# Two more chunk pairs of the first FFN in Strassen's form, and half a query chunk ahead of the product with Wo in the second attention

## The chip, the cores and the metric

The kernel runs on one core of a Trainium2 chip. The metric is the time of one execution on the device, in microseconds; before the change the median of three runs is 401.58 us (401.27 to 401.74). Engines are named as in the profile: PE is TensorE's matmuls and PEld its weight loads, DVE is VectorE, ACT is ScalarE, POOL is GpSimd, SP is SyncE, which issues transfers.

## What is computed

The input x has 2048 tokens of 512 numbers. It goes through an attention block A, a feed-forward block B, A again and B again, with the same weights both times:

```python
def A(x):                                  # 32 heads of 16, linear attention
    q, k, v = split(x @ wqkv)              # wqkv 512 x 1536
    phi = lambda t: where(t > 0, t + 1, exp(t)) + 1e-6
    kv  = einsum("bhsd,bhse->bhde", phi(k), v)
    z   = phi(k).sum(tokens)
    num = einsum("bhqd,bhde->bhqe", phi(q), kv)
    den = einsum("bhqd,bhd->bhq", phi(q), z) + 1e-6
    return (num / den) @ wo
def B(x):                                  # 512 -> 1792 -> 512
    return (silu(x @ w_gate) * (x @ w_up)) @ w_down

x = x + A(layernorm(x)); x = x + B(layernorm(x))
x = x + A(layernorm(x)); x = x + B(layernorm(x))
```

## The kernel before

**Tiling.** Everything stays in SBUF. Tokens are 16 tiles of 128, four tiles to a group (0 to 3). The layers are numbered 0 (first attention), 1 (first FFN), 2 (second attention) and 3 (second FFN). Matmuls read bf16 and add up in eight PSUM banks of 512 columns.

**Tokens of the program.** The string PROGRAM, a table written by hand, is the order of TensorE's work, token by token: layer digit, a letter, and indices. Those that matter here:
- `1u212`: chunk 12 (128 of the 1792 hidden features) of group 2 in layer 1, direct: eight matmuls of 512 columns, four with Wg and four with Wu (`gu`). ACT takes silu of the first bank, DVE multiplies by the second. Late chunks, those behind the first key of layer 2, take the silu by way of tanh, with one more DVE instruction.
- `1y251`: product 1 of 7 of Strassen's form for a pair of chunks, here 5 and 12 (j and j + 7), of group 2 (`gs`). A pair is two chunks by two halves of the group (256 tokens each) by two halves of the 512 inputs; seven products of 4 matmuls of 256 columns (two for the gate, two for up) take the place of 16 matmuls of 512. Products 1, 6 and 7 share one growing bank, which ACT copies out after each (`cp`, line 1248), and products 2, 3 and 5 add a bank to such a copy on DVE (`ca`, line 1227); then ACT takes silu of the gate half (`sih`, line 1219) and POOL multiplies (`hp`, line 1242). Product 4 needs a silu on ACT and a product on DVE (`hh`, line 1258).
- `1p16`: a piece of the product with Wd (`down`), in Strassen's form too, for which DVE adds blocks of h (`1h1.sb1`, line 1322, into RT).
- `2k0`: keys of token tile 0 in layer 2 (four matmuls of 512). `2q10`: query chunk 0 of group 1 (four of 512). `2Q30`: half of query chunk 0 of group 3 early (four of 256, `q_first`); the later `2q30` is then the other half. `U` is the same for an FFN chunk.
- After a query chunk, `phi` runs: ACT's exponential into etmp (`exp`, line 700), DVE's min and add on etmp (`ts`, line 705), and the last step into pq on DVE (`phi`, line 709 or 712), for some chunks after a copy with bias on ACT (`id1`, line 703).
- `2v`: sixteen matmuls of 128 columns that give the masked product of keys and values (`kvt`): the block diagonal is cut out by DVE in two instructions (`mask` and `mask1`, line 809), each for a half, into KVT, which lies in the buffer etmp. `2m0` to `2m3`: that times Wo, one matmul each (`m_mm`); `2m0` and `2m1` need the first half, `2m2` and `2m3` the second.
- `2d10`: a piece of the denominators (Zm by pq, 8 columns); after the fourth, ACT takes the logarithm into dsb and then, for group 1 of layer 2, the reciprocals into rtok (`2d1.rxs`, line 878), which DVE transposes into rT (`2d1.dT`, line 886). `2r1`: sixteen small matmuls with esel that spread them over the features (`rep_pe`); DVE multiplies pq by the result (line 933). For other groups ACT spreads them (`rex`, line 896, into rrep or hT), SP transposes by DMA into RT, and DVE or POOL multiply (`pqn`, line 915). `2w4`: the product of pq with the combined matrix for tile 4 (`wo`).

**Weight pieces.** Strassen's form reads sums of blocks of Wg and Wu (`1W2.ws6` and the like, POOL, line 1101), made once for each two chunks, and sums of blocks of the tokens (`1gx3.xs`). The sums lie where Wqkv and Wo lay. When the last product that reads them is through, `reload` has POOL's queue load Wqkv again in four transfers: two for the keys (`R.ldk`, `R.ldk1`, 256 KB each), one for the queries (`R.ldq`, 512 KB), one for the values (`R.ldv`, 512 KB). The keys of layer 2 read the first two, its queries the third.

**Order of the other engines.** ORDER is a dictionary with one string of operation names for each of ACT, DVE, POOL and SP, written by hand: each engine issues in just that order, and waits for semaphores that the kernel derives from what an operation reads and writes. An operation that waits holds up all that stands behind it on its engine. ON_ACT is a set of names that moves operations between engines.

Of the kernel before, what the change touches and what calls it, by code (L numbers as in the profile page):

```python
# [1588 lines left out]
```

## Time and profile before

| | us |
|---|---|
| median of 3 runs | 401.58 (401.27 to 401.74) |
| the profiled execution | 401.14 |
| its span on the core | 399.4 |
| PE busy | 394.3 (99%) |
| DVE busy | 327.5 (82%) |
| ACT busy | 268.8 (67%) |
| POOL busy | 214.5 (54%) |

The granted clock of TensorE is full (1.00) over the whole span. The profile is of one execution; the 1.7 us between its span and its time lie around the program. The chain of work that ended last is 97% matmuls. A PE row's duration has a modelled end; the start of the next row, where nothing is waited for, tells how long the engine was held.

### The profile page before, as it was taken

Reading aid. Unit: us, or ns where it says so; the run is one execution under the profiler, and the core shown is the slowest. Engines: PE = TensorE matmul, PEld = TensorE weight load, DVE = VectorE, ACT = ScalarE, POOL = GpSimd, SP = SyncE. Lnnn points to the kernel's source line nnn. Section 1 sums busy time; section 2 is a strip of 40 time slices with the busy share of each in tenths; the row PEclk is TensorE's granted clock in tenths of the full one; section 3 lists DMA queues with packets and bytes.
Section 4 is the critical chain, followed back from the end, with each engine's and each line's share of the span. In section 5 each row is a group of like instructions: output and inputs, shape, how many; then the busy total and the mean of one; then the engine's idle time right before and its main releaser. Section 6 shows DMA issues by size and latency. Waiting matters only on the chain.

```text
span 399.4 us, 7922 instructions
## 1 busy us (share of the span) xinstructions
PE 394.3 (99%) x2922; PEld 264.5 (66%) x2922; DVE 327.5 (82%) x785; ACT 268.8 (67%) x569; POOL 214.5 (54%) x352
## 2 busy tenths in 40 slices
PE   7999999999999999999999999999999999999997
PEld 6444555445787787565786445454588888888886
DVE  5996599377987779699997666987698889899997
...
DMA packets 53783, 25.43 MB, mean 64 GB/s; under 512 B 46512, under 2 KB 52144, under 8 KB 53744
## 3 DMA queue, kind: packets, MB, share of 16 engines
...
q10 hardware_dynamic: 544, 0.52, 0.4%
q8 instruction: 23, 0.38, 0.4%
...
## 4 chain that ended last, share of the span: by engine, by line
PE 97%; DMA 1%; DVE 1%; ACT 0%; issue 0%; SPq 0%; DVEq 0%
PE pb L492 97%; DMA X<-in_A_x_dram 1%; DVE pq L1442 0%; PE pb L679 0%; ACT xnA L624 0%; ACT xnA L616 0%; DVE stats L609 0%; DVE etmp L809 0%; SPq L535 0%; DVEq L1559 0%; DVE xnA L655 0%; DVE mv L611 0%; DVE vpe L640 0%; DVE xnA L1368 0%
## 5 line engine op out<-in xcount | busy, mean ns | idle before, releaser
L492 PE MATMUL pb<-xnT,Wg 128*128 128x512 bf16 (+1 forms) x332 | 75.3, 334 | 0.0
L492 PE MATMUL pb<-xnT,Wu 128*128 128x512 bf16 (+1 forms) x332 | 75.3, 334 | 0.0
L1242 POOL TENSOR_TENSOR hT<-pq 128x256 bf16<-128x256 f32 x45 | 34.1, 769 | 45.4 <-ACT pq L1219 45.3
L1248 ACT ACTIVATE pq<-pb 128x512 f32<-128x512 f32 x63 | 36.6, 594 | 28.2 <-PE pb L492 24.8
L492 PEld LDWEIGHTS pb<-xnT,Wu 128*128 128x128 bf16 x332 | 32.5, 98 | 24.2
L1227 DVE TENSOR_TENSOR pq<-pb,pq 128x512 f32<-128x512 f32 x63 | 41.9, 682 | 5.7 <-PE pb L492 2.9
L492 PEld LDWEIGHTS pb<-xnT,Wg 128*128 128x128 bf16 x332 | 32.3, 98 | 21.2 <-DMA xnT<-xnB 0.2
L1018 DVE TENSOR_TENSOR hT<-tht,pb 128x512 bf16<-128x512 f32 x46 | 30.8, 681 | 17.2 <-ACT tht L1013 12.2
L644 POOL TENSOR_TENSOR rstd<-vpe,negh 128x1 f32<-128x1 f32 x62 | 36.5, 590 | 9.5 <-DVE vpe L640 7.3
L1013 ACT ACTIVATE tht<-pb 128x512 f32<-128x512 f32 x46 | 26.4, 594 | 22.5 <-PE pb L492 21.5
L492 PE MATMUL pb<-Wd,hT 128*128 128x256 bf16 x336 | 40.3, 273 | 0.0
L700 ACT ACTIVATE etmp<-pb 128x512 bf16<-128x512 f32 x64 | 36.7, 601 | 3.8 <-PE pb L492 2.9
L492 PEld LDWEIGHTS pb<-Wd,hT 128*128 128x128 bf16 x336 | 32.9, 98 | 4.2
L492 PE MATMUL pb<-pk,xnA 128*128 128x512 bf16 (+1 forms) x152 | 34.7, 362 | 0.0
L492 PE MATMUL pb<-xnT,Wqkv 128*128 128x512 bf16 (+1 forms) x132 | 32.8, 376 | 0.0
L705 DVE TENSOR_SCALAR etmp<-etmp 128x512 bf16<-128x512 bf16 x64 | 19.4, 314 | 15.5 <-ACT etmp L700 15.5
L492 PE MATMUL pb<-Wqkv,xnT 128*128 128x512 bf16 x128 | 30.8, 379 | 0.0
L1219 ACT ACTIVATE pq<-pq 128x256 f32<-128x256 f32 x63 | 24.9, 411 | 8.1 <-DVE pq L1227 8.0
L492 PE MATMUL pb<-GT,pq 128*128 128x512 bf16 x128 | 29.9, 379 | 0.0
L624 ACT ACTIVATE etmp<-X,sums 128x512 bf16<-128x512 bf16 x32 | 22.9, 715 | 5.0 <-DVE X L945 3.8
L628 POOL TENSOR_SCALAR mv<-sums 128x1 f32<-128x1 f32 x52 | 14.1, 275 | 21.2 <-DVE X L945 12.5
L945 DVE SCALAR_TENSOR_TENSOR X<-pb,X 128x512 bf16<-128x512 f32 x32 | 21.1, 681 | 3.5 <-PE pb L492 3.4
...
## 6 DMA issues: line engine op xcount, KB each, us to landing
...
Wqkv<-in_A_wqkv_dram SPq DMA_DIRECT2D x2, 512.0 KB, 7.4
Wo<-in_A_wo_dram POOLq DMA_DIRECT2D x2, 512.0 KB, 4.6
Wqkv<-in_A_wqkv_dram POOLq DMA_DIRECT2D x2, 512.0 KB, 5.1
```

The costliest lines, as they stand in the source:

```text
L492: return op("pe", lambda e: e.matmul(o_ap, lhsT=lhsT, rhs=rhs, start=start, stop=stop, skip_group_check=skip), r=r, w=w, n=n)
L624: op("act", lambda a: a.activation(out=sq_ap, in_=X[:, t, :], func=ACT.Square, scale=-float(D), bias=sums[:, t:t + 1], accum_out=mv[:, t, ...
L644: op("pool", lambda p: p.tensor_tensor(out=rstd[:, t:t + 1], in0=vpe[:, t:t + 1], in1=negh[:], op=ALU.pow), r=[f"vp{t}", "negh"], w=[f"rs{ ...
L700: exps.append(op("act", lambda a: a.activation(out=etmp[e][:], in_=PB[pb], func=ACT.Exp), r=[f"pb{pb}"], w=[f"e{e}"], after=silus, kind="e ...
L705: op("dve", lambda v: v.tensor_scalar(out=etmp[e][:], in0=etmp[e][:], scalar1=1.0, scalar2=1e-6, op0=ALU.min, op1=ALU.add), r=[f"e{e}"], w ...
L945: op("dve", lambda v: v.scalar_tensor_tensor(out=X[:, t, :], in0=PB[pb], scalar=1.0, in1=X[:, t, :], op0=ALU.mult, op1=ALU.add, accum_out= ...
L1013: silus.append(op("act", lambda e: e.activation(out=tht[a][:], in_=PB[pg], func=ACT.Silu), r=[f"pb{pg}"], w=[f"th{a}"], after=exps, kind=" ...
L1018: op("dve", lambda v: v.tensor_tensor(out=hT[h][:, j, :], in0=tht[a][:], in1=PB[pu], op=ALU.mult), r=[f"pb{pu}", f"th{a}"], w=hk, kind="h")
L1219: silus.append(op("act", lambda e: e.activation(out=o_ap, in_=i_ap, func=ACT.Silu), r=r, w=w, after=exps, kind="sih" if len(w) == 1 else " ...
L1227: op("dve", lambda v: v.tensor_tensor(out=c, in0=PB[b], in1=c, op=ALU.add), r=[f"pb{b}", k], w=[k], kind="ca")
L1242: lambda e: e.tensor_tensor(out=hT[h][:, jj, o:o + 256], in0=c[:, 0:256], in1=c[:, 256:512], op=ALU.mult),
L1248: op("act", lambda e: e.activation(out=c, in_=PB[pb], func=ACT.Copy), r=pk_, w=[k], kind="cp")
```

## The change

Four things change, all in tables; no function does.

1. PROGRAM loses the chunks 1u212, 1u205 (group 2), 1u304 and 1u311 (group 3), and gains the fourteen products 1y251 to 1y257 and 1y341 to 1y347, that is the pairs (5, 12) of group 2 and (4, 11) of group 3. They stand between 1u303 and 2k0, woven into what was there; the two chunks of group 3 stood behind 2k0 before. The last product that reads the piece sums in Wqkv's place is 1y343 now; it was 1y243.
2. PROGRAM gains 2Q30 between 2v and 2m0; one bank is held from there until 2q30.
3. The four strings of ORDER get the new operations, and many neighbours change places, in layers 0 and 3 too.
4. ON_ACT gains 1c303, which moves nothing here, since the buffer it needs is lent out.

```diff
-1u303 1y243 1u212 1u306 1u205 1u309 1y301 1y311 1u302 1y306 1u310 1y316 1y315 1y307 1y305 1u313 1y317 1y304 1y302
-1y312 1y303 1y313 1y314 2k0 2k1 2q10 2k4 1u304 2k3 2k2 2k6 1p21 2q01 2k5 1u305 1p26 1p22 1p27 1p25 1u311 1p24 1u312
...
+1u303 1y251 1y243 1y252 1y256 1y345 1u306 1y255 1y257 1y341 1u309 1y253 1y301 1y342 1y254 1y346 1y311 1u302 1y306
+1u310 1y347 1y315 1y316 1y344 1y307 1y343 1y305 1u313 1y317 1y304 1y302 1y312 1y303 1y313 1y314 2k0 2k1 2q10 2k4 2k3
...
-2d22 2d23 2g4 2d11 2d12 2g1 2d13 2q33 2v 2m0 2m1 2m3 2m2 2r1 2w3 2w2 2w0 2w1 2q30 2q32 2w4 2d31 2w6 2w8 2w7 2w10 2d33
+2d22 2d23 2g4 2d11 2d12 2g1 2d13 2q33 2v 2Q30 2m0 2m1
+2m3 2m2 2r1 2w3 2w2 2w0 2w1 2q30 2q32 2w4 2d31 2w6 2w8 2w7 2w10 2d33 2w9 2d30 2d32 2w11 2w5 3U008 3u008 3u001 3u004
...
     "dve": """
-0d0.pqn 0q30.ts 0v.mask 0v.mask1 0q30.phi 0q31.ts 0M2.evac 0q31.phi 0d1.pqn1 0q33.ts 0w1.res 0d2.dT 0w2.res 0q33.phi
+0d0.pqn 0v.mask 0q30.ts 0v.mask1 0q30.phi 0q31.ts 0M2.evac 0q31.phi 0d1.pqn1 0q33.ts 0w1.res 0d2.dT 0w2.res 0q33.phi
```

The first place is TensorE at the masked product of the second attention: GT with Wqkv is 2v, Wo with etmp are 2m0 to 2m3, rT with esel is 2r1. Before:

```order
L492 MATMUL pb<-xnT,Wqkv 128x512 x4
L492 MATMUL pb<-GT,Wqkv 128x128 x16
L492 MATMUL pb<-Wo,etmp 128x512 x4
L492 MATMUL pb<-rT,esel 128x128 x16
L492 MATMUL pb<-GT,pq 128x512 x16
L492 MATMUL pb<-xnT,Wqkv 128x512 x8
```

After:

```order
L495 MATMUL pb<-xnT,Wqkv 128x512 x4
L495 MATMUL pb<-GT,Wqkv 128x128 x16
L495 MATMUL pb<-xnT,Wqkv 128x256 x4
L495 MATMUL pb<-Wo,etmp 128x512 x4
L495 MATMUL pb<-rT,esel 128x128 x16
L495 MATMUL pb<-GT,pq 128x512 x16
L495 MATMUL pb<-xnT,Wqkv 128x256 x4
L495 MATMUL pb<-xnT,Wqkv 128x512 x4
```

Four matmuls of 256 columns moved ahead of the product with Wo, and the query chunk behind is halved by as much.

On DVE at the same place, the two mask instructions, the min and add of query chunk 2q33 (L705), the transpose rT and the evacuations of Wo's product (CAST), before:

```order
L809 TENSOR_TENSOR etmp<-pb,mask 128x256 x2
L886 STREAM_TRANSPOSE rT<-rtok 128x128
L705 TENSOR_SCALAR etmp<-etmp 128x512
L798 CAST GT<-pb 128x512
L933 TENSOR_TENSOR pq<-pq,pb 128x16x32
L709 TENSOR_TENSOR pq<-pq,etmp 128x512
```

After:

```order
L812 TENSOR_TENSOR etmp<-pb,mask 128x256
L708 TENSOR_SCALAR etmp<-etmp 128x512
L812 TENSOR_TENSOR etmp<-pb,mask 128x256
L712 TENSOR_TENSOR pq<-pq,etmp 128x512
L889 STREAM_TRANSPOSE rT<-rtok 128x128
L801 CAST GT<-pb 128x512
```

The step of 2q33 on etmp went between the two masks and its last step ahead of the transpose. On ACT 2q33.id1 went ahead of 2d1.rxs.

The second place is DVE at the masked product of the first attention: L915 is 0d0.pqn, L705 is 0q30.ts, then the two masks and 0q30.phi. Before:

```order
L798 CAST GT<-pb 128x512 x2
L915 TENSOR_TENSOR pq<-pq,RT 128x4x128
L705 TENSOR_SCALAR etmp<-etmp 128x512
L809 TENSOR_TENSOR etmp<-pb,mask 128x256 x2
L712 SCALAR_TENSOR_TENSOR pq<-pb,etmp 128x512
```

After:

```order
L801 CAST GT<-pb 128x512 x2
L918 TENSOR_TENSOR pq<-pq,RT 128x4x128
L812 TENSOR_TENSOR etmp<-pb,mask 128x256
L708 TENSOR_SCALAR etmp<-etmp 128x512
L812 TENSOR_TENSOR etmp<-pb,mask 128x256
L715 SCALAR_TENSOR_TENSOR pq<-pb,etmp 128x512
```

The first mask went ahead of 0q30.ts. On ACT at that place one of the copies of 0d1 into rrep (0d1.rex) went ahead of the exponential 0q30.exp.

The third place is POOL at the reload of Wqkv (the DMA rows), ahead of the keys of layer 2. Before:

```order
L1242 TENSOR_TENSOR hT<-pq 128x256
L535 DMA Wqkv<-in_A_wqkv_dram 128x2x512 x2
L628 TENSOR_SCALAR mv<-sums 128x1
L1242 TENSOR_TENSOR hT<-pq 128x256
L535 DMA Wqkv<-in_A_wqkv_dram 128x4x512 x2
L640 TENSOR_SCALAR vpe<-mv 128x1
L1242 TENSOR_TENSOR hT<-rrep 128x256
```

After:

```order
L1245 TENSOR_TENSOR hT<-pq 128x256
L538 DMA Wqkv<-in_A_wqkv_dram 128x2x512 x2
L538 DMA Wqkv<-in_A_wqkv_dram 128x4x512 x2
L1245 TENSOR_TENSOR hT<-rrep 128x256
L538 DMA Wo<-in_A_wo_dram 128x4x512
L1245 TENSOR_TENSOR hT<-pq 128x256 x5
```

The four loads stand in one piece, and wait for 1y343 where they waited for 1y243.

## Rows read from the trace of the kernel before

**Rows 1.** The page, part 1: busy time, share of the span, instructions of each engine.

```profile
PE 394.3 (99%) x2922; PEld 264.5 (66%) x2922; DVE 327.5 (82%) x785; ACT 268.8 (67%) x569; POOL 214.5 (54%) x352
```

**Rows 2.** Busy time by stretch: us, then busy (instructions) of each engine, clock, DMA.

```profile
core 0: us, PE busy (x) PEld busy (x) DVE busy (x) ACT busy (x) POOL busy (x), PEclk, DMA share, GB/s
156.13:176.49 20.36, 20.36 (x126) 12.14 (x124) 15.12 (x33) 13.60 (x30) 17.33 (x28) 1.00 0.49 124
```

**Rows 3.** Timeline of PE: start, duration, engine, line, operation, [idle before <-releaser].

```profile
169.96 1.91 PE L492 MATMUL pb<-Wo,pk 128*128 128x256 bf16 x16
171.71 1.03 PE L492 MATMUL pb<-xnT,Wg 128*128 128x512 bf16 x4
172.57 1.03 PE L492 MATMUL pb<-xnT,Wu 128*128 128x512 bf16 x4
```

**Rows 4.** The page, part 5, POOL's products of halves: busy, mean ns, idle before.

```profile
L1242 POOL TENSOR_TENSOR hT<-pq 128x256 bf16<-128x256 f32 x45 | 34.1, 769 | 45.4 <-ACT pq L1219 45.3
```

**Rows 5.** Timeline at a product that waited for a copy.

```profile
153.50 0.60 ACT L1248 ACTIVATE rrep<-pb 128x512 f32<-128x512 f32 x1 [1.36 <-PE pb L492]
...
154.15 0.11 PEld L492 LDWEIGHTS pb<-pk,Wg 128*128 128x128 bf16 x2 [0.15 <-ACT rrep L1248]
```

**Rows 6.** Timeline of PE at the masked product of the second attention.

```profile
245.92 1.06 PE L492 MATMUL pb<-GT,Wqkv 128*128 128x128 bf16 x16
247.14 1.02 PE L492 MATMUL pb<-Wo,etmp 128*128 128x512 bf16 x4 [0.16 <-DVE etmp L809]
248.09 0.40 PE L492 MATMUL pb<-rT,esel 32*128 32x128 bf16 x16
```

**Rows 7.** Timeline of DVE and ACT at the same place.

```profile
246.57 0.87 DVE L809 TENSOR_TENSOR etmp<-pb,mask 128x256 bf16<-128x256 f32 x2 [0.77 <-PE pb L492]
246.63 0.33 ACT L878 ACTIVATE rtok<-dsb 128x128 bf16<-128x128 f32 x1
246.83 0.71 ACT L703 ACTIVATE pq<-pb,onep 128x512 bf16<-128x512 f32 x1
...
247.36 0.30 DVE L886 STREAM_TRANSPOSE rT<-rtok 128x128 bf16<-128x128 bf16 x1
...
247.58 0.25 DVE L705 TENSOR_SCALAR etmp<-etmp 128x512 bf16<-128x512 bf16 x1
```

**Rows 8.** Timeline of all engines at the masked product of the first attention.

```profile
49.87 1.27 POOL L915 TENSOR_TENSOR pq<-pq,RT 128x512 bf16<-128x512 bf16 x1 [1.94 <-DMA RT<-hT]
...
49.92 1.06 PE L492 MATMUL pb<-GT,Wqkv 128*128 128x128 bf16 x16
...
50.51 0.62 ACT L896 ACTIVATE rrep<-dsb 128x512 bf16<-128x512 f32 x1
50.65 0.64 DVE L705 TENSOR_SCALAR etmp<-etmp 128x512 bf16<-128x512 bf16 x1 [0.52 <-ACT etmp L700]
...
50.82 1.03 PE L492 MATMUL pb<-xnT,Wqkv 128*128 128x512 bf16 x4
...
51.68 0.35 PE L492 MATMUL pb<-Zm,pq 128*128 128x8 bf16 x8
...
52.10 1.02 PE L492 MATMUL pb<-Wo,etmp 128*128 128x512 bf16 x4
```

**Rows 9.** Timeline of DVE, POOL and PE at the sums of h in group 2.

```profile
136.01 1.27 DVE L1322 TENSOR_TENSOR RT<-RT,hT 128x1024 bf16<-128x1024 bf16 x2
...
137.84 1.15 POOL L1101 TENSOR_TENSOR Wqkv<-Wu 128x512 bf16<-128x512 bf16 x1
...
139.05 0.38 PE L492 MATMUL pb<-Td,RT 128*128 128x256 bf16 x2
```

**Rows 10.** Timeline at the reload; the third load's landing; landings of all four.

```profile
157.86 0.60 PE L492 MATMUL pb<-xnT,Wqkv 128*128 128x256 bf16 x4
...
158.76 1.53 POOL L535 DMA_DIRECT2D Wqkv<-in_A_wqkv_dram  x2 [0.23 <-PE pb L492]
...
Wqkv<-in_A_wqkv_dram POOLq DMA_DIRECT2D x1, 512.0 KB, 4.8
...
DMA to landing us min/median/max: 3.9/4.4/5.5
```

More of the change, by code (lines that the diff above doesn't have):

```diff
@@ new lines @@
+0k11.id1 0q02.id1 0q02.exp 0k12.exp 0k12.id1 0q23.exp 0q22.id1 0q22.exp 0d0.ln 0d0.rex1 0d0.rex3 0q21.exp 0q10.id1
+0d0.rex 0q10.exp 0d0.rex2 0q20.exp 0d1.ln 0d1.rex3 i.c1 0d1.rex1 0G2.evac 0G3.evac 0d1.rex 0q30.exp 0d1.rex2 0q31.exp
+0M3.evac 0M0.evac 0M1.evac 0q33.exp 0d2.ln 0d2.rxs 0q33.id1 1x1.sq 1x2.sq 1x3.sq 1x2.apply 0q32.exp 1x0.sq 1x3.apply
+1x4.sq 1x5.sq 1x7.sq 1x6.sq 1x4.apply 1u012.silu 0d3.rep1 1u000.silu 1x9.sq 1x11.sq 1u001.silu 1x7.apply 1u007.silu
+0d3.rep 1u011.silu 1u004.silu 1u005.silu 0d3.rep3 1u006.silu 1u003.silu 1x6.apply 1x10.sq 1u010.silu 0d3.rep2
@@ new lines @@
+1y305.sih 1y317.sih 1y343.sih 1y304.sih 1y342.sih 1y314.sih 1y302.sih 1y347.sih 1y313.sih 2k0.id1 1y312.sih 1y303.sih
+2k1.exp 2k0.exp 2k4.id1 2q10.exp 2k2.id1 2k3.exp 2k4.exp 2k3.id1 2k2.exp 2q01.id1 2k6.exp 2k5.exp 2k5.id1 2q01.exp
+1u305.tanh 2k6.id1 1u312.tanh 2x11.sq 2x10.sq 2x11.apply 2k7.id1 2x8.sq 2x9.sq 2k7.exp 2x10.apply 2k11.exp 2x9.apply
+2q02.exp 2x15.sq 2x14.sq 2q12.exp 2q12.id1 2q00.exp 2x13.sq 2x12.sq 2k9.exp 2k9.id1 2x13.apply 2k10.id1 2k8.exp
+2k10.exp 2k8.id1 2k15.id1 2k15.exp 2k14.exp 2q11.id1 2k13.exp 2q11.exp 2k13.id1 2k12.exp 2k12.id1 2q31.id1 2q20.id1
@@ new lines @@
+2q21.id1 2q31.exp 2q20.exp 2q21.exp 2q03.id1 2q03.exp 2d0.ln 2d0.rex1 2d0.rex3 2q13.exp 2d0.rex 2q23.exp 2q23.id1
+2q22.id1 2q22.exp 2d0.rex2 2d2.ln 2d2.rex1 2d2.rex 2G2.evac 2G3.evac 2d1.ln 2q33.exp 2q33.id1 2d1.rxs 2M0.evac
+2M1.evac 2M2.evac 2d2.rex3 2d2.rex2 3x3.sq 3x2.sq 2q30.exp 3x0.sq 2q32.exp 3x1.sq 3x0.apply 3x4.sq 3x8.sq 3x6.sq
+3x9.sq 3x7.sq 3x6.apply 2d3.rep 2d3.rep1 3u008.silu 3x11.sq 3u001.silu 3u010.silu 2d3.rep2 3u004.silu 3x7.apply
+2d3.rep3 3x10.sq 3x5.sq 3u005.silu 3u000.silu 3x12.sq 3u009.silu 3u002.silu 3x5.apply 3x15.sq 3u012.silu 3u007.silu
@@ new lines @@
+1y205.ca 1h1.sa2 1p15.uu 1y233.ca 1y234.hh 1p17.uu 2x0.apply 1p17.rh 1p12.rh 1p17.rh1 1p12.rh1 1y203.ca 1y204.hh
+1p13.rh 1y245.ca 1p13.rh1 2x2.apply 1y242.ca 1p13.tot 1p14.rh1 1y244.hh 1u303.h 2x4.tot 2x6.tot 1y243.ca 1p14.rh
+1y252.ca 2x7.vpe 2x4.vpe 1h2.sb 1p14.tot 1y257.ca 1u306.h 1u309.h 1y253.ca 1y342.ca 2x4.apply 2x5.apply 1y254.hh
+1h2.sb3 1u302.h 2x7.apply 1y347.ca 1h2.sa 1h2.sb1 1u310.h 1y344.hh 1y305.ca 1y343.ca 1h2.sa1 1y317.ca 1u313.h 1h2.sb2
+1y304.hh 1y302.ca 1y313.ca 1y312.ca 1y303.ca 1h2.sa2 1y314.hh 2k1.ts 1h2.sa3 2k0.ts 2k1.phi 2k0.phi 2q10.ts 2k0.zs
@@ new lines @@
+2q10.phi 1p21.uu 2k4.ts 2k4.phi 2k2.ts 2k1.zs 2k2.phi 2k4.zs 2k6.ts 2k3.ts 2k5.ts 2k3.phi 2k5.phi 1p26.uu 1u305.gst
+2q01.ts 1u305.h 1p22.rh 1p27.uu 2k6.phi 1p22.rh1 1p25.rh 1h3.sb 2k6.zs 1p24.rh 1p25.rh1 2k5.zs 1p24.rh1 1u312.gst
+1p24.tot 1u312.h 2q01.phi 1h3.sa 2x10.tot 1h3.sb1 1h3.sa1 1p31.uu 1p23.rh 1p23.rh1 1h3.sb2 2x8.tot 2x10.vpe 1p23.tot
+1h3.sa2 1h3.sb3 1p36.uu 1h3.sa3 2k7.ts 1p36.uu1 1p33.rh 2k7.phi 2x8.apply 1p37.uu 1p37.rh1 2k11.ts 2k11.phi 1p37.rh
+1p34.rh1 2x14.tot 1p33.rh1 1p34.rh 2q02.ts 2x15.vpe 1p34.tot 1p32.rh1 2x15.apply 2x12.tot 1p32.rh 2x14.vpe 2q02.phi
@@ new lines @@
+2q12.ts 1p32.tot 2x14.apply 2q00.ts 2q00.phi 2k9.ts 2x12.apply 2k9.phi 2q12.phi 2k10.ts 2k10.phi 2k15.ts 2k8.ts
+2k14.ts 2k8.phi 2k15.phi 2k14.phi 2k13.ts 2k13.phi 2k14.zs 2k12.ts 2q11.ts 2k13.zs 2k12.phi 2q11.phi 2k12.zs 2s.zh
+2s.zl 2q31.ts 2q31.phi 2q21.ts 2z.zm 2q21.phi 2q03.ts 2q20.ts 2q20.phi 2q03.phi 2q13.ts 2q23.ts 2q13.phi 2q22.ts
+2q22.phi 2q23.phi 2d0.pqn 2d0.pqn1 2G0.evac 2G1.evac 2v.mask 2q33.ts 2v.mask1 2q33.phi 2d1.dT 2M3.evac 2r1.pqn 2d2.pqn
+2w3.res 2r1.pqn1 2w2.res 2r1.pqn2 3x3.apply 2r1.pqn3 2w0.res 3x2.apply 2q30.ts 2d2.pqn3 2w1.res 2q30.phi 2d2.pqn2
```

257 lines of the change are left out of this document (115 added, 142 removed).

## The prediction

> **What bounds the kernel now.** The page comes first: TensorE is busy 394.3 of 399.4 us [rows 1]. A change is therefore worth what it takes from TensorE's own work, plus what it opens or closes of the few gaps in it. The busy time by stretch comes next: from 156.13 to 176.49 us, where the two pairs change form, TensorE is busy 20.36 of 20.36 us at the full clock (1.00), while POOL has 17.33, DVE 15.12 and ACT 13.60 [rows 2]. No engine beside it is full, and none of them makes it wait there. So I price the pairs by TensorE's own step, and then look in the timelines for the gaps that the rewritten order tables touch.
>
> The profiled execution took 401.14 us, 0.44 us less than the median, 401.58. All differences below are worked out against the trace of that execution; I set the total against the median, since the median is what will be compared.
>
> **A, the two pairs.** Each pair loses two chunks of 8 matmuls of 512 columns and gains 7 products of 4 matmuls of 256 columns. Where four matmuls of 512 columns follow sixteen of 256 without a gap, the sixteen take from 169.96 to 171.71 us, 1.75 us or 0.1094 each, and the four from 171.71 to 172.57, 0.215 each [rows 3]. A pair goes from 16 x 0.215 = 3.44 to 28 x 0.1094 = 3.06 us, so -0.38, and the two pairs give **-0.77 us**. The sums of weight pieces that the products read are made already for pairs of other groups, and the sums of token blocks too, so nothing else comes with them on TensorE.
>
> The cost lies on the other engines. From 1u303 to 2k0 the stretch gets 14 products (6.13 us) for two chunks (3.44 us); the other two chunks leave a later place. It becomes 20.36 + 2.69 = 23.05 us long. POOL gets six products of halves at 0.769 us [rows 4]: 17.33 + 4.61 = 21.9 of 23.05. ACT gets six copies at 0.60 us [rows 5] and eight silus of half a bank, for two silus of a whole one; at 0.60 us each these 12 net are 7.2, so at most 20.8. DVE gains six instructions net; at 1 us each it would still have 21.1. TensorE's work covers all of it, POOL the most narrowly; the cover fails only where one wait is too tight by itself.
>
> **D, waits inside the new products.** Before, a product waited once for the copy that frees a bank: the copy began at 153.50, took 0.60 us, and the weight load behind it shows 0.15 us without work [rows 5]. Weights are loaded ahead of their matmuls, so a part of that is covered by matmuls still running. I find two such places in the new order (1y256 behind 1y251, 1y344 behind 1y347), and take **+0.10**, a third of the most: between 0 (all covered) and 0.30 (twice 0.15).
>
> **B, the gap after the masked product.** Sixteen matmuls of 128 columns take 0.90 us where nothing stops them, from 49.92 to 50.82 [rows 8]. From 245.92 they are thus through at 246.82, and the product with Wo begins at 247.14 [rows 6]: 0.32 us lost behind the mask on DVE, which is two instructions, 0.87 us together from 246.57 [rows 7]. The new half of a query chunk is 4 x 0.1094 = 0.44 us. It fills the gap and pushes the product with Wo 0.12 us later; the other half of the chunk is 0.44 shorter later on. Net -0.32 if nothing else comes late. But DVE now has 2q33.ts between the two masks and 2q33.phi behind them, and ACT does 2q33.id1, 0.71 us, ahead of the reciprocals in rtok, 0.33 us, which it did first before [rows 7]. So rtok is ready not at 246.96 but near 247.67, and the transpose rT (0.30 us) ends near 248.0 to 248.15; the matmuls that read it stood at 248.09 [rows 6] and now stand at 248.21. The margin is 0.05 to 0.2 us. I take **-0.28**, between -0.32 and -0.15.
>
> **C, the same place in the first attention.** The sixteen matmuls at 49.92 are shown as 1.06 us though the next begins after 0.90, so a row's modelled end lies 0.16 too late. The x8 group of small matmuls at 51.68, shown as 0.35, is then through near 51.88, and the product with Wo begins at 52.10 [rows 8]. The 0.22 us are lost behind DVE: its tensor-scalar step on etmp (0q30.ts) took 0.64 us from 50.65, where the same step in layer 2 took 0.25 [rows 7], and both masks queue behind it. Beside it POOL multiplied pq by RT from 49.87 for 1.27 us, that is until 51.14 [rows 8], and the step ended soon after that. The new order puts the first mask ahead of the step, and ACT a copy into rrep (0.62 us, [rows 8]) ahead of the exponential that the step waits for. The step then starts 0.5 to 0.6 us later, at 51.15 to 51.25, when POOL is done, lasts about 0.25, and the second mask (half of 0.87) ends between 51.8 and 51.95, where 51.88 is wanted. I take **-0.18**, between -0.22 and +0.07 (if the step still takes 0.64).
> [...]
>
> **E, POOL's piece sums moved up.** In group 2 the sums of h on DVE, two instructions of two SBUF inputs, 1.27 us from 136.01, are read by TensorE at 139.05 [rows 9]. POOL's sums of weight pieces, 1.15 us each, came after them (137.84); the new order has two of them ahead of two products of halves, so that they may run beside the sums. The margin is 139.05 - 137.28 = 1.77 us; two whole waits of 1.15 would overrun it by 0.53. I weight it low, since one of the two waits alone is covered. I take **+0.10**, between 0 and 0.53.
>
> The remaining swaps in the tables are of neighbours away from any gap; I count them nothing, covered by TensorE's work as in [rows 2]; without that cover one such swap costs a step of some 0.2 us, which the range holds.
>
> Sum: -0.77 + 0.10 - 0.28 - 0.18 + 0.10 = **-1.03 us**: 400.11 for the profiled execution, 400.55 for the median, which I give as 400.5. All good ends together give -0.77 + 0 - 0.32 - 0.22 = -1.31, so 400.3.
>
> **Rivals.**
> *The locks stay (400.9 to 401.4).* If 0q30.ts is still held and the sums of E collide, C is +0.07 and E 0.25 to 0.53: -0.77 + 0.10 - 0.28 + 0.07 + 0.25 = -0.63, so 400.95, up to 401.25 with 0.53, and 401.4 with the worst B. For it: the 0.64 itself, and two sums of two SBUF inputs each with POOL's long ones moved up to them. Against it: the new order of DVE and ACT takes this one step off POOL's span.
>
> *The reload comes late (up to slower than before).* The piece sums lie where Wqkv was, and its reload by POOL's queue waits for the last product that reads them. That was 1y243, whose four matmuls begin at 157.86 and end near 158.30; the first load was issued at 158.76, two in 1.53 us [rows 10]. There were 18 us until 2k0. Now it is 1y343, and behind it TensorE has only eight products and one chunk, 8 x 0.4376 + 1.72 = 5.22 us, until 2k0; 2k0 and 2k1 are eight matmuls of 512, so 2q10 stands at 5.22 + 1.72 = 6.94. The third load, for 2q10, is issued 0.46 + 1.53 = 2.0 us behind 1y343 and took 4.8 us to land, so 6.8; the longest of the four took 5.5, so 7.5 [rows 10]. That is between 0.1 early and 0.6 late. With 0.55 late the sum is -0.5: 401.1. It makes the kernel slower than before only if the third load lands over 8.0 us behind 1y343 (6.0 from issue), and by more than 0.2% from 6.8; at 7.5 from issue it gives 2.5 late, 403.1. Against it: 4.8 for this very load, and no landing over 5.5. For it: four issues in a row instead of two and two, and so little cover.
> [...] No row here shows a landing longer than 5.5 us, with DVE busy three quarters of that stretch.
>
> *The pairs bring nothing (401.3 or more).* They do so if a product's step is 32 x 0.215 / 56 = 0.123 us and not 0.109; every row of 256 columns in the stretch stands at 0.109 [rows 3], so this needs a new gap of 0.38 us in each pair.
> [...]
>
> **How the numbers follow.** 0.2% of 401.58, about what a measurement of this kernel can tell from no change, is 0.80 us: faster is below 400.78, slower above 402.38. Forecast, 400.5, itself between 400.3 and 400.8: 0.60. Locks stay, 400.8 to 401.4: 0.24. Reload late by up to 0.6 us, near 401.1: 0.08; later, above 402.4 in most of it: 0.06. Pairs bring nothing: 0.02. Faster is most of the first case, 0.57; slower the late reload, 0.06; the rest, 0.37, is the same. The range goes from 400.1 (the good ends, less 0.2 for the spread of a median) to 401.4.
>
> **What would show it.** A: the 1y25x and 1y34x products 0.4376 us apart, each pair some 0.38 us shorter; wrong if DVE or POOL become the releaser of TensorE there. B: no idle time before the product with Wo after 2v, and the esel matmuls within 0.1 us of their queue. C: 0q30.ts at 0.3 us and no idle time ahead of Wo's product near 51.9. D: weight loads behind a copy into a temporary. E: the length of the two sums near 136 us, and a wait of the matmuls on RT. Reload: TensorE's wait for Wqkv before 2k0 or 2q10. The forecast is wrong as a whole if TensorE's busy time doesn't fall by about 0.8 us.

## The result, and the profile after

The changed kernel takes 406.22 us (median of 5 runs, 403.65 to 408.11) against 401.54 us for the kernel before in the same runs. The ratio is 1.0114, with a 95% interval of 1.0073 to 1.0155: slower by 1.1%, where 0.3% faster was forecast. Its profiled execution has a span of 404.7 us, 5.3 us more than before.

The waits of TensorE by what ended them (us in total, times, longest) show one that the kernel before does not have. Before, then after:

```profile
PE pb L492 <- DVE hT L498: 1.2, 1, 1.2
PE pb L679 <- DVE xnA L655: 0.8, 1, 0.8
PE pb L492 <- DVE etmp L809: 0.2, 1, 0.2
```

```profile
PE pb L495 <- DVE X L948: 3.0, 1, 3.0
PE pb L495 <- DVE hT L501: 1.2, 1, 1.2
PE pb L495 <- DVE pq L1230: 0.4, 1, 0.4
PE pb L495 <- DMA xnT<-xnB: 0.2, 1, 0.2
PE pb L495 <- DVE etmp L812: 0.2, 1, 0.2
PE pb L495 <- ACT GT L798: 0.2, 1, 0.2
```

The 3.0 us lie at the start of the first FFN, 90 us ahead of the first of the two pairs. In the timeline of that place, PE first, then DVE, then POOL:

```profile
70.90 1.03 PE L495 MATMUL pb<-xnT,Wu 128*128 128x512 bf16 x4
74.89 1.64 PE L495 MATMUL pb<-xnT,Wg 128*128 128x512 bf16 x4 [2.97 <-DVE X L948]
76.32 1.91 PE L495 MATMUL pb<-xnT,Wu 128*128 128x512 bf16 x4
...
69.67 4.56 DVE L658 TENSOR_SCALAR xnB<-X,mv,rstd 128x512 bf16<-128x512 bf16 x1 [0.58 <-POOL rstd L647]
74.15 0.68 DVE L948 SCALAR_TENSOR_TENSOR X<-pb,X 128x512 bf16<-128x512 f32 x1
...
67.98 0.80 POOL L538 DMA_DIRECT2D Wd<-in_B_w_down_dram  x1 [1.65 <-DMA xnT<-xnB]
68.83 0.27 POOL L651 TENSOR_SCALAR nmr<-mv,rstd 128x1 f32<-128x1 f32 x1
69.06 0.57 POOL L647 TENSOR_TENSOR rstd<-vpe,negh 128x1 f32<-128x1 f32 x1
69.61 2.25 POOL L1104 TENSOR_TENSOR xnA<-Wg 128x512 bf16<-128x512 bf16 x2
71.82 1.14 POOL L1104 TENSOR_TENSOR pk<-Wu 128x512 bf16<-128x512 bf16 x1
72.93 1.14 POOL L1104 TENSOR_TENSOR xnA<-Wu 128x512 bf16<-128x512 bf16 x1
```

The DVE row of 4.56 us is 1x5.apply, the normalization of one token tile. In the kernel before it met one sum of POOL's and took 0.41 us:

```profile
68.71 1.15 POOL L1101 TENSOR_TENSOR xnA<-Wg 128x512 bf16<-128x512 bf16 x1
69.68 0.41 DVE L655 TENSOR_SCALAR xnB<-X,mv,rstd 128x512 bf16<-128x512 bf16 x1
```

In the changed kernel it starts when the scale of the tile (1x5.pow, L647 on POOL) is there, and ends at 74.23, just behind the fourth of four sums of weight pieces that stand in a row on POOL (72.93 + 1.14 = 74.07). Behind it on DVE stands 0w8.res (L948), the last reader of the PSUM bank that the chunk 1u007 wants; so TensorE stood for 2.97 us. After that stop the granted clock falls. The view of busy time by stretch (us; then busy time of PE, PEld, DVE, ACT, POOL with instructions; clock; DMA) has

```profile
72.00:75.00 3.00, 0.11 (x1) 0.11 (x2) 3.00 (x4) 2.75 (x7) 2.96 (x4) 1.00 0.00 0
75.00:79.00 4.00, 4.00 (x12) 1.41 (x12) 2.44 (x6) 1.65 (x3) 3.82 (x9) 0.57 0.88 167
```

At the granted clock of 0.57 the four matmuls from 76.32 take to 78.03, 0.43 us each instead of 0.215 [rows 3]. From 74.89 to 79.18 twelve matmuls take 4.29 us instead of 2.58, so 1.7 us more. Of the five runs one kept the full clock, and it is the fastest (403.65); the others show a mean clock of 0.992 or 0.996.

Where the whole difference lies is read from the starts of TensorE's work, counted from the first matmul of 0g2 so that the start of the program, which varies by some 0.7 us between the executions, drops out (us; three experiments beside):

| first matmul of | before | after | a_clean | b_pairs | b_half |
|---|---|---|---|---|---|
| 1u000 | 54.32 | 54.69 | 54.42 | 54.38 | 54.29 |
| 1u011 | 61.22 | 66.42 | 61.33 | 61.28 | 61.20 |
| 1u303 | 142.67 | 147.86 | 142.77 | 142.72 | 142.64 |
| 2k0 | 163.03 | 171.00 | 165.91 | 165.86 | 163.00 |
| 2q10 | 164.76 | 173.25 | 168.12 | 168.12 | 164.73 |
| 2g2 | 204.28 | 209.32 | 204.19 | 204.27 | 204.26 |
| 2v | 232.45 | 237.49 | 232.36 | 232.44 | 232.43 |
| 3u008 | 248.44 | 253.40 | 248.27 | 248.43 | 248.49 |
| end of the last matmul | 383.23 | 388.39 | 383.06 | 383.22 | 383.28 |

By differences of a column: +0.37 up to 1u000, +4.83 from there to 1u011, -0.01 to 1u303, -0.15 from 1u303 to 2g2 (both pairs and the reload are in it), nothing to 2v, -0.08 to 3u008 (the half chunk), +0.20 to the end; the sum is +5.16. The pairs, the reload and the half chunk, which the prediction was mostly about, moved the time by a quarter of a microsecond. What it counted at nothing, the swaps of neighbours in the order tables, cost 4.8 between 1u000 and 1u011.

### The profile page after: what moved, and what is told of

Its sections match the earlier page's. It is cut to its first block, busy times and chain, and to the rows that moved or that the text cites. A ratio compares the mean times of both kernels' runs of the same rounds, so it can differ in the third digit from the quotient of the medians.

```text
span 404.7 us, 7992 instructions
## 1 busy us (share of the span) xinstructions
PE 396.5 (98%) x2950; PEld 268.3 (66%) x2950; DVE 333.5 (82%) x787; ACT 272.6 (67%) x579; POOL 219.9 (54%) x358
## 4 chain that ended last, share of the span: by engine, by line
PE 89%; DVE 4%; issue 2%; ACT 2%; DMA 2%; POOL 0%; SPq 0%; DVEq 0%; POOLq 0%
PE pb L495 89%; DMA xnT<-xnB 1%; ACT GT L798 1%; DMA X<-in_A_x_dram 1%; DVE pq L936 1%; DVE X L948 1%; DVE pq L1230 0%; DVE pq L1445 0%; DVE xnB L658 0%; DVE etmp L708 0%; POOL rstd L647 0%; ACT etmp L703 0%; PE pb L682 0%; ACT xnA L627 0%; ACT xnA L619 0%
## 5 line engine op out<-in xcount | busy, mean ns | idle before, releaser
L495 PE MATMUL pb<-xnT,Wg 128*128 128x512 bf16 (+1 forms) x324 | 73.7, 334 | 3.2 <-DVE X L948 3.0
L495 PE MATMUL pb<-xnT,Wu 128*128 128x512 bf16 (+1 forms) x324 | 73.6, 333 | 0.0
L1245 POOL TENSOR_TENSOR hT<-pq 128x256 bf16<-128x256 f32 x48 | 35.6, 754 | 47.4 <-ACT pq L1222 47.4
L1251 ACT ACTIVATE pq<-pb 128x512 f32<-128x512 f32 x66 | 38.7, 596 | 32.8 <-PE pb L495 27.7
L1230 DVE TENSOR_TENSOR pq<-pb,pq 128x512 f32<-128x512 f32 x66 | 44.3, 683 | 7.9 <-ACT pq L1251 4.5
L1021 DVE TENSOR_TENSOR hT<-tht,pb 128x512 bf16<-128x512 f32 x44 | 29.6, 682 | 16.0 <-PE pb L495 10.3
L647 POOL TENSOR_TENSOR rstd<-vpe,negh 128x1 f32<-128x1 f32 x62 | 36.3, 588 | 11.5 <-DVE vpe L643 9.0
L495 PE MATMUL pb<-xnT,Wqkv 128*128 128x512 bf16 (+1 forms) x144 | 34.2, 364 | 0.4 <-DVE pq L1230 0.4
L948 DVE SCALAR_TENSOR_TENSOR X<-pb,X 128x512 bf16<-128x512 f32 x32 | 21.4, 684 | 5.3 <-PE pb L495 5.3
```

The source lines that it names most:

```text
L495: return op("pe", lambda e: e.matmul(o_ap, lhsT=lhsT, rhs=rhs, start=start, stop=stop, skip_group_check=skip), r=r, w=w, n=n)
L647: op("pool", lambda p: p.tensor_tensor(out=rstd[:, t:t + 1], in0=vpe[:, t:t + 1], in1=negh[:], op=ALU.pow), r=[f"vp{t}", "negh"], w=[f"rs{ ...
L948: op("dve", lambda v: v.scalar_tensor_tensor(out=X[:, t, :], in0=PB[pb], scalar=1.0, in1=X[:, t, :], op0=ALU.mult, op1=ALU.add, accum_out= ...
L1021: op("dve", lambda v: v.tensor_tensor(out=hT[h][:, j, :], in0=tht[a][:], in1=PB[pu], op=ALU.mult), r=[f"pb{pu}", f"th{a}"], w=hk, kind="h")
L1230: op("dve", lambda v: v.tensor_tensor(out=c, in0=PB[b], in1=c, op=ALU.add), r=[f"pb{b}", k], w=[k], kind="ca")
L1245: lambda e: e.tensor_tensor(out=hT[h][:, jj, o:o + 256], in0=c[:, 0:256], in1=c[:, 256:512], op=ALU.mult),
```

## The experiments

The theory at the start: a DVE instruction that meets a row of POOL's sums is held until the whole row is through, and all that stands behind it on DVE with it. The rival: 1x5.apply is merely released late (its reciprocal now stands behind the issue of Wd.ld2), and 0w8.res stands behind it on DVE. Later kernels test what is left once the front is mended. Kernels that begin with a_ are made from the changed one, those with b_ from the one before. Where two kernels differ by less than a median can tell, I use one length of the profiled execution, from DVE's 0q23.phi (39 us into the program) to DVE's last instruction: 358.08 us before, 363.10 after. It is one execution of each kernel: a_clean and a_early, which have the same orders up to the pairs, differ by 0.14 us in the first attention, so a difference of that size says nothing.

### a_apart and a_small: what stands beside 1x5.apply

a_apart, on POOL:

```diff
-1x4.nmr 1x5.pow 1W1.ws 1W1.ws2 1W0.ws6 1W1.ws4 Wd.ld 1x11.negm 1x6.vpe 1x7.negm 1x7.pow
+1x4.nmr 1x5.pow Wd.ld 1x11.negm 1x6.vpe 1x7.negm 1W1.ws 1W1.ws2 1W0.ws6 1W1.ws4 1x7.pow
```

> The changed kernel with one edit on POOL: the issue of Wd.ld and three operations of one column (1x11.negm, 1x6.vpe, 1x7.negm) go ahead of the four weight-piece sums 1W1.ws, 1W1.ws2, 1W0.ws6, 1W1.ws4, so that DVE's 1x5.apply, which the reciprocal just before releases, meets no sum when it starts. Theory 'row of sums': 1x5.apply takes 0.4 to 0.6 us instead of 4.56, TensorE's 3.1 us without work at the start of the FFN and the half clock behind it (1.9 us) go, and the time is 401.0 to 401.7. Rival 'late release': 1x5.apply is late because its reciprocal now stands behind Wd.ld2, and 0w8.res stands behind it; that is not undone here, so the stall stays above 2 us and the time above 404.

a_small, on POOL:

```diff
-1x5.pow 1W1.ws 1W1.ws2 1W0.ws6
+1x5.pow 1W1.ws 1x11.negm 1W1.ws2 1W0.ws6
```

> The changed kernel with one edit on POOL: 1x11.negm, an operation of one column (0.2 to 0.3 us), stands between the first and the second of the four sums in a row. Theory 'row of sums, held without a break': DVE gets in only where POOL works on something small, so 1x5.apply ends 0.1 to 0.4 us after the first sum, takes 1.3 to 1.8 us, and the stall goes: 401.0 to 402. Theory 'row held to its end': the small one makes no difference, 1x5.apply takes 4.7 to 5 us, the time is 405 to 408. If POOL let go after every sum, 1x5.apply would not have taken 4.56 us in the first place.

The row of 1x5.apply in a_apart, then in a_small:

```profile
69.58 0.41 DVE L658 TENSOR_SCALAR xnB<-X,mv,rstd 128x512 bf16<-128x512 bf16 x1 [0.46 <-POOL rstd L647]
```

```profile
69.15 4.77 DVE L658 TENSOR_SCALAR xnB<-X,mv,rstd 128x512 bf16<-128x512 bf16 x1 [0.69 <-POOL rstd L647]
...
69.09 1.14 POOL L1104 TENSOR_TENSOR xnA<-Wg 128x512 bf16<-128x512 bf16 x1
70.21 0.23 POOL L631 TENSOR_SCALAR mv<-sums 128x1 f32<-128x1 f32 x1
70.41 1.15 POOL L1104 TENSOR_TENSOR xnA<-Wg 128x512 bf16<-128x512 bf16 x1
```

Without sums beside it the instruction takes 0.41 us, at the same lateness; with them, and a short operation of one column between, 4.77. So the late release alone does not make the instruction long, the sums do, and here it is held to the end of the row: the short operation opens nothing. a_small runs at 407.13 us (1.0138, 1.0110 to 1.0166), as its second theory said.

a_apart was expected at 401.0 to 401.7 and came out at 406.06 (1.0111, 1.0082 to 1.0141), above 404 as the rival had it, but not for the rival's reason. The wait at 1u007 is gone; another has taken its place 10 us later. In its timeline, PE, DVE and POOL:

```profile
80.52 1.03 PE L495 MATMUL pb<-xnT,Wg 128*128 128x512 bf16 x4
84.42 1.89 PE L495 MATMUL pb<-xnT,Wu 128*128 128x512 bf16 x4 [2.88 <-DVE hT L1021]
...
80.37 3.40 DVE L591 TENSOR_TENSOR Td<-Wd 128x512 bf16<-128x512 bf16 x1
...
79.89 0.77 POOL L538 DMA_DIRECT2D Wd<-in_B_w_down_dram  x1
80.68 1.16 POOL L1104 TENSOR_TENSOR pk<-Wg 128x512 bf16<-128x512 bf16 x1
81.79 0.58 POOL L647 TENSOR_TENSOR rstd<-vpe,negh 128x1 f32<-128x1 f32 x1
82.33 1.14 POOL L1104 TENSOR_TENSOR pk<-Wu 128x512 bf16<-128x512 bf16 x1
```

Wd.tw4 on DVE, with two SBUF inputs, took 3.40 us (0.42 in the kernel before) beside another row of POOL's, and the product of h behind it kept 1u003 from its bank for 2.88 us; the four matmuls behind that stop take from 84.42 to 86.11, 0.42 us each, and the mean clock of the execution is 0.996. The front of the changed kernel has two such places, and the first hid the second: in the changed kernel itself Wd.tw4 took 1.89 us and nothing waited. The expectation of the time was wrong because I mended one place and looked at no other.

### b_row: the row alone, on the kernel before

```diff
-1x5.negm 1x5.pow 1x4.vpe 1x4.pow 1x4.negm Wd.ld2 1x4.nmr 1W1.ws 1x7.negm Wd.ld 1x7.pow 1W1.ws4 Wd.ld1 1W0.ws6 1W1.ws2 1W0.ws
+1x5.negm 1x4.vpe 1x4.pow 1x4.negm Wd.ld2 1x4.nmr 1x5.pow 1W1.ws 1W1.ws2 1W0.ws6 1W1.ws4 1x7.negm Wd.ld 1x7.pow Wd.ld1 1W0.ws
```

> The kernel before with one edit on POOL: 1x5.pow goes behind Wd.ld2 and 1x4.nmr, and the sums 1W1.ws, 1W1.ws2, 1W0.ws6, 1W1.ws4 stand in a row behind it, as in the changed kernel; DVE's order stays, with 0w8.res ahead of 1x5.apply. Theory 'row of sums': 1x5.apply takes 4 to 4.6 us instead of 0.41, the first products of h stand behind it, and TensorE waits 1.5 to 2.5 us for a bank at 1u004 instead of 1u007, with some loss of clock perhaps: 403 to 405. Rival 'late release' (the place of 0w8.res decides): no wait above 0.3 us, 401.4 to 401.9.

```profile
70.20 4.11 DVE L655 TENSOR_SCALAR xnB<-X,mv,rstd 128x512 bf16<-128x512 bf16 x1
```

402.88 us, 1.0038 (1.0025 to 1.0052). With DVE's order untouched the hold is there in full, 4.11 us, and TensorE waits 1.0 us for a product of h behind it; the mean clock is 1.000. So the row alone makes the kernel slower, by less than I had put (a wait of 1.5 to 2.5 us): with 0w8.res ahead of the held instruction one bank more is free. Of the 4.8 us, 1.7 are the lower clock; that the place of 0w8.res makes up the rest is by subtraction, since no run moves it alone.

### a_front and a_clean: the old front under the pairs

a_front takes ACT's, DVE's, POOL's and SP's orders from the kernel before up to the pairs; a_clean differs from it on SP alone:

```diff
-2x1.xT 2x3.xT 2x4.xT 2x0.xT 2x5.xT 2x6.xT 2x2.xT 2x7.xT
+2x0.xT 2x1.xT 2x2.xT 2x3.xT 2x4.xT 2x5.xT 2x6.xT 2x7.xT
```

> The changed kernel, with ACT's, DVE's, POOL's and SP's orders taken from the kernel before up to the pairs (1y242.sih, 1y244.hh, 1y213.hp, 2x7.xT), so with the pairs, the half query chunk and all that follows. If the loss lies in the reordered front alone, what is left is -0.77 for the pairs, -0.1 for the half chunk, +0.5 for the wait before 2q10 and +0.2 for one near the end: 401.0 to 401.7. If the pairs or the half chunk cost more than the trace of the changed kernel shows, it is above 402.

> The changed kernel with ACT's, DVE's and POOL's orders of the kernel before up to the pairs, as in a_front, but with SP's transposes in the changed kernel's order from 2x1.xT on (2x0 and 2x2 early), so that none is issued beside the reload of Wqkv. Theory 'the reload is slowed by the transpose beside it': the four landings come back to 3.1 to 6 us from issue (a_front had 4.1 to 7.4), 2k0 waits no 1.6 us for R.ldk1, about 0.3 to 0.5 us stay before 2q10, and the time is 1.2 to 1.7 below a_front: 400.4 to 401.2. Rival 'DVE holds up the reload': the landings stay above 5.9 us for R.ldk1 and the time at 402.

a_front: 402.15 us, 1.0015 (1.0005 to 1.0025). The start of the FFN is as before, so the reordered front was the loss. But the reload came late. The first row is its PE timeline at 2k0, the second the landings of its four loads; the last are those of a_clean:

```profile
181.46 1.47 PE L495 MATMUL pb<-Wqkv,xnT 128*128 128x512 bf16 x6 [1.42 <-DMA Wqkv<-in_A_wqkv_dram]
...
DMA to landing us min/median/max: 4.1/6.3/7.4
```

```profile
DMA to landing us min/median/max: 3.1/4.2/5.9
```

In a_front a transpose (2x7.xT) is issued in the middle of the four loads, 0.7 us behind the first; in a_clean it is issued 2.8 us ahead of them. The landings are shorter by 1.0 to 2.6 us, 2k0 waits no more, and the time is 400.87 us, 0.9991 (0.9982 to 1.0000): about the kernel before, 0.2 us faster in the table above. DVE's order is the same in both, so it is not DVE that held up the reload there.

### b_pairs and b_half: the two parts alone

b_pairs has the fourteen products with their operations in the changed kernel's order between 1y242 and 2k0, and SP's order of a_clean; all else is as before. b_half is one word:

```diff
-2q33 2v 2m0 2m1
+2q33 2v 2Q30 2m0 2m1
```

> The kernel before with the two pairs alone: the fourteen products on TensorE and their operations on ACT, DVE and POOL in the changed kernel's order between 1y242 and 2k0 (SP's transposes 2x0 and 2x2 early as in a_clean), no half query chunk, all other orders as before. The pairs' own gain is -0.77, the wait before 2q10 gives back 0.3 to 0.5: 401.0 to 401.4, against 401.5. If the smaller matmuls brought nothing, 401.8 to 402.2.

> The kernel before with 2Q30 alone, all orders of the other engines as before. The gap of 0.33 us before 2m0 goes. Theory 'a bank is short': since one bank is held for the half chunk, 2w3 takes the bank that 2M1.evac reads and waits 0.2 to 0.35 us for it, so that 0.0 to 0.15 us are left: 401.3 to 401.5. If only the later transpose rT had cost in the changed kernel, here, where ACT and DVE keep their order, the gain is 0.3: 401.15 to 401.25.

b_pairs: 401.24 us, 1.0003 (0.9994 to 1.0011). From 1u303 to 2k0 it takes 23.14 us, 2.78 more than before; the prediction had 2.69 and 0.10 for small waits. The two chunks that stood behind 2k0 are 3.45 us. But 2q10 starts 2.25 us behind 2k0 and not 1.73: a wait of 0.53. The pairs win 0.67 and lose 0.53 at once, and 0.07 at a transpose later.

b_half: 401.56 us, 1.0011 (1.0002 to 1.0020). The gap before 2m0 is gone (0.33 us), yet from 2v to 3u008 it takes 16.06 us instead of 15.99. 2w3 now waits 0.34 us and not 0.09: in after, a_clean and b_half alike it begins 0.14 us after ACT's 2M1.evac has ended, in the kernel before 0.28 us after 2M0.evac, one evacuation earlier. That fits the held bank, since 2w3 takes the bank that was read longest ago, and with one of eight held that is 2M1's. A product of 2w5 waits 0.14 us too. With the changed orders (after, a_clean) the same stretch takes 15.91, so there the half chunk is worth 0.08.

### a_cover, a_early, b_early, a_chunk and a_swap: cover for the reload

In five kernels with the pairs (after, a_clean, b_pairs, a_small, a_front) 2q10 begins 0.24 us after the third load has landed, to 0.01 us. The profile names DVE's 1y312.ca for that wait; but in a_small that instruction ended 0.19 us after 2q10 had begun, and in a_apart, where the load landed after 4.4 us and not 5.0 to 6.7, 2q10 did not wait. So the reload is the releaser, and the name in the row is that of another that came close.

```diff
# a_cover (on a_clean): TensorE, then DVE
-2k0 2k1 2q10 2k4
+2k0 2k1 2k4 2q10
-1h2.sb2 1y304.hh 1y302.ca 1y313.ca 1y312.ca 1y303.ca
+1y304.hh 1y302.ca 1y313.ca 1y312.ca 1y303.ca 1h2.sb2
# a_early (on a_clean) and b_early (on b_pairs): TensorE
-1y316 1y344 1y307 1y343
+1y316 1y343 1y344 1y307
# a_chunk (on a_clean): TensorE; on ACT and DVE 1u305's silu and product likewise
-1y314 2k0
+1y314 1u305 2k0
# a_swap (on a_clean): POOL
-R.ldk R.ldk1 R.ldq R.ldv
+R.ldk R.ldq R.ldk1 R.ldv
```

> As a_clean, with two edits: 2k4 goes ahead of 2q10 on TensorE (0.86 us more cover for the third load of the reload and for the bank that 2q10 needs), and DVE's sum 1h2.sb2 goes behind 1y303.ca, so that the bank comes free 0.68 us earlier. Theory 'thin cover behind 1y343': the wait of 0.3 to 0.5 us before 2q10 goes, and the time is 0.3 to 0.5 below a_clean: 400.0 to 400.8, faster than both. Rival: the wait moves to 2q10's or 2k3's next need, and the time equals a_clean's within 0.2.

> a_clean with one edit: product 1y343, the last reader of the piece sums in Wqkv's place, goes ahead of 1y344 and 1y307, so that the reload starts 0.87 us earlier against 2k0 and 2q10. In five of seven runs with the pairs 2q10 began 0.24 us after the third load had landed, whether the bank's last reader on DVE was through or not. Theory 'the reload is late': 2q10's wait of 0.49 us falls to 0 to 0.1, and from the first key sums (0g2) to the last matmul TensorE takes 0.4 to 0.5 us less than a_clean's 383.06: time 400.3 to 400.6. Rival 'the bank is late' (the profile names DVE's 1y312.ca): DVE's order is the same, so 2q10's wait stays at 0.4 to 0.5 and the time at 400.9. Second rival: the earlier reload runs beside the transpose 2x7.xT, its landings grow by 1 to 2 us as in a_front, and the time is above 401.3.

> b_pairs (the kernel before with the two pairs alone) with 1y343 ahead of 1y344 and 1y307. The pairs' own gain without the late reload: the wait before 2q10 goes from 0.53 to at most 0.1 us, and TensorE from 0g2 to its end takes 382.65 to 382.85 us against 383.23 before and 383.22 in b_pairs: time 400.6 to 400.9. If the pairs were worth nothing, it stays at 383.2.

> a_clean with the chunk 1u305 ahead of 2k0 instead of behind 2k5 (its silu is then plain, and one DVE instruction goes): 1.73 us more cover for the reload without moving the reload. Theory 'the reload is late': no wait before 2q10, 0.4 to 0.5 below a_clean, 400.3 to 400.6. Rival: what 1u305 covered behind 2k5 (banks and DVE there) is uncovered, a wait of 0.5 us or more comes up between 2k5 and 1p27, and the time is 400.9 or more.

> a_clean with one edit on POOL: the third load of the reload (R.ldq, for 2q10) is issued ahead of the second (R.ldk1, for the third matmul of 2k0). In a_clean R.ldk1 landed 1.1 us before it was wanted, R.ldq 0.25 too late. Theory 'the reload alone keeps the gain back': R.ldq lands 0.75 us earlier, R.ldk1 0.7 to 0.9 later and still in time; the wait of 0.49 us before 2q10 goes and nothing comes in its place; from 0q23.phi to DVE's last instruction 357.4 to 357.6 us instead of 357.90 (before: 358.08); time 400.4 to 400.7. Rival: R.ldk1 queues behind the 512 KB of R.ldq and makes 2k0 wait 0.3 us or more, or DVE's backlog behind 2k0 takes the gain: 357.8 or more.

| | us | ratio (interval) | 0q23.phi to the end | the wait that took the place |
|---|---|---|---|---|
| a_clean | 400.87 | 0.9991 (0.9982 to 1.0000) | 357.90 | 2q10 on the reload, 0.49 |
| a_cover | 402.46 | 1.0033 (1.0021 to 1.0046) | 359.25 | 1u305 on 2k4.exp 1.1, 1p27 on DVE 0.5 |
| a_early | 401.25 | 0.9992 (0.9983 to 1.0001) | 358.21 | 1y343 on DVE 0.54 |
| b_early | 401.97 | 1.0016 (1.0007 to 1.0024) | 358.80 | 1y343 on DVE 0.5 |
| a_chunk | 401.37 | 1.0001 (0.9992 to 1.0010) | 357.99 | 1p27 on DVE 0.6 |
| a_swap | 401.79 | 1.0009 (1.0000 to 1.0017) | 358.31 | 2k0 on the second load, 0.9 |

In each the wait before 2q10 went, and in each another came up that was as long or longer: all five failed in what they were for. In a_early the row is plain. Product 3 adds to the bank that 1y347.ca has to read first, and moved ahead it waits for just that:

```profile
173.44 0.61 PE L495 MATMUL pb<-xnT,Wqkv 128*128 128x256 bf16 x4 [0.54 <-DVE pq L1230]
```

In a_swap the 512 KB issued ahead of the second load made that one land after 4.6 us instead of 3.3. So the pairs' gain is not kept back by one wait that an edit takes away. The stretch behind 2k0 had DVE at 22.5 of 23.9 us in the kernel before, and what is taken out of it, or moved, uncovers the next thing.

### a_mask, b_mask, a_best and a_cmask: the masks of the first attention

```diff
-0v.mask 0q30.ts 0v.mask1 0q30.phi
+0v.mask 0v.mask1 0q30.ts 0q30.phi
```

The cut is against the changed kernel. The four kernels are made from a_early (a_mask), a_swap (a_best), a_clean (a_cmask) and the kernel before (b_mask); in each of those 0q30.ts stood ahead of both masks, as before, and the edit puts it behind both.

> a_early with one edit on DVE, in the first attention: 0q30.ts goes behind both masks, so that neither mask queues behind an operation that POOL's product holds up. Theory 'row held by POOL, masks free of it': 0q30.ts still takes 0.5 to 0.8 us, the masks 0.43 each, and the wait of 0.2 to 0.4 us before 0m3 goes; 0.2 to 0.35 below a_early. Rival: the masks themselves are held, or the late 0q30.ts makes 0d30 wait, and nothing is won (within 0.1 of a_early).

> The kernel before with that edit alone. Theory: the wait of 0.22 us before 0m3 goes, nothing else moves: 357.8 to 357.9 us from 0q23.phi to DVE's last instruction, time 0.15 to 0.25 below before. Rival: within 0.1 of before.

> a_swap with the edit of a_mask (0q30.ts behind both masks on DVE). The wait of 0.2 to 0.4 us before 0m3 goes too: 357.0 to 357.4 us from 0q23.phi to DVE's last instruction, 0.7 to 1.1 less than the kernel before; time 400.1 to 400.5, faster than both kernels.

> a_clean with the one edit of a_mask: on DVE 0q30.ts goes behind both masks in the first attention. Theory 'the step is held by POOL, the masks are not': both masks take 0.42 us each, the wait of 0.38 us before 0m3 goes, and from 0q23.phi to DVE's last instruction it takes 357.4 to 357.7 us (a_clean 357.90, before 358.08): time 400.3 to 400.8. Rival: the transfers of the transposes for 0d1, which vary from run to run, end later than the masks and take the gain: 357.9 or more.

In a_cmask, on POOL, DVE and PE:

```profile
49.71 1.41 POOL L918 TENSOR_TENSOR pq<-pq,RT 128x512 bf16<-128x512 bf16 x1 [1.79 <-DMA RT<-hT]
...
50.55 0.87 DVE L812 TENSOR_TENSOR etmp<-pb,mask 128x256 bf16<-128x256 f32 x2 [0.44 <-PE pb L495]
...
51.34 0.28 DVE L708 TENSOR_SCALAR etmp<-etmp 128x512 bf16<-128x512 bf16 x1
...
51.86 1.02 PE L495 MATMUL pb<-Wo,etmp 128*128 128x512 bf16 x4
```

The masks run beside POOL's product at their own 0.87 us, and the product with Wo waits for nothing. a_mask takes 0.21 us off a_early (357.99 to the end of DVE, time 400.97 us, 0.9987, 0.9978 to 0.9996); 0q30.ts took 0.28 and not the 0.5 to 0.8 that I had expected, since it started when POOL was done. b_mask takes 0.26 off the kernel before in the trace (357.82), which its times do not show (401.18 us, 0.9999, 0.9990 to 1.0008). a_best missed its 400.1 to 400.5 (401.56 us, 1.0008, 0.9999 to 1.0017): the wait of 2k0 on the second load, 0.9 us, stands in it as in a_swap, and in its profiled execution DVE also waited 1.0 us for a transfer into RT, so that its length (359.12) says nothing of the edit.

a_cmask is the version to keep: 400.66 us against 401.22, 0.9978 (0.9969 to 0.9988), 357.29 us in the trace. It is faster than the kernel before by 0.2% (by the ratio; the two medians alone give 0.9986), and 1.4% faster than the changed one. Not all of its 0.61 us against a_clean in the trace come from the masks: at the start of the FFN it is 0.37 ahead, and the other 0.24 come at 2q10, which again begins 0.24 us behind the third load's landing, but that load landed earlier in this execution (4.97 us from issue, 5.20 in a_clean).

## Why the prediction was wrong, point by point

**The swaps counted at nothing.** This is the step that failed: "covered by TensorE's work", with a price of 0.2 us for one swap without cover. Two swaps met: POOL's 1x5.pow went behind a load's issue, which released 1x5.apply just as four sums began that had been brought together in a row, and 0w8.res went behind 1x5.apply. The listings of the order showed each of them. No row quoted from the trace of before showed the sum of them, but [rows 8] showed a step on DVE lengthened beside one operation of POOL's (0.64 us, against 0.25 in [rows 7]), and I looked for that at C and E only. The cost is 4.8 us: 3.1 without work and 1.7 at the lower clock, so the time lies 4.8 us above the top of the range, 401.4.

**The locks, as a rival.** That an instruction of DVE is held beside one of POOL's was in the prediction with the right sign, at the wrong places and with the wrong size. I priced a held instruction at one POOL operation, 1.15 us. At the start of the FFN it is held for a row of them: 4.56, 4.77 and 4.11 us beside four sums, 3.40 beside two sums with a short operation between. Four sums finished one after another before DVE went on. It is not so in every row: the last section has two where one instruction was the whole hold (0.83 and 0.77 us).

**A, the pairs.** Right in size: -0.67 with the small waits of D, against -0.77 + 0.10. But 0.53 came back at 2q10 at once, so that b_pairs is worth nothing that can be measured. The sign set for the forecast as a whole, TensorE's busy time lower by about 0.8 us, did not come: it rose from 394.3 to 396.5 in the changed kernel, which the lower clock is part of, and was 394.1 in a_clean.

**D, small waits.** 0.04 us at 1y256 and 0.07 at 1y344, together about the 0.10 taken.

**The reload.** The rival given 8 in 100 is what happened: in the changed kernel the third load landed 0.28 us late, and the matmul began 0.24 after the landing, 0.52 in all, inside the 0 to 0.6 worked out from [rows 10]. Its chance was far too low. The row showed 0.1 us of margin with nothing for the way from landing to the first matmul.

**B, the half chunk.** Forecast -0.28, measured -0.08 with the changed orders and +0.07 alone. The gap went as described. What I left out is the bank: the text of the change says that one is held, and I did not ask who takes which bank next.

**C, the first attention's masks.** Forecast -0.18, measured +0.15. In the changed kernel:

```profile
50.60 1.15 POOL L918 TENSOR_TENSOR pq<-pq,RT 128x512 bf16<-128x512 bf16 x1 [2.46 <-DMA RT<-hT]
...
51.19 0.71 DVE L708 TENSOR_SCALAR etmp<-etmp 128x512 bf16<-128x512 bf16 x1
...
51.82 0.41 DVE L812 TENSOR_TENSOR etmp<-pb,mask 128x256 bf16<-128x256 f32 x1
...
52.38 0.38 PE L495 MATMUL pb<-Wo,etmp 128*128 128x512 bf16 x1 [0.23 <-DVE etmp L812]
```

I took POOL's product at its time of before, and it waits for a transfer, which ended later; so it held 0q30.ts again, with the second mask behind it. The mechanism was right, as a_cmask shows; the half of the edit that left the step between the masks was not enough.

**E, the sums in group 2.** POOL held them as feared, 2.11 us together instead of 1.27 [rows 9], and the margin of 1.77 us covered it: no cost.

**Not foreseen and small.** A wait of 0.4 us at 1u012 for a transpose (0.09 before), and one of 0.2 us near the end for a sum of h that DVE's new order puts later.
